# Attention scores by heads and weight transposes by token halves, each in one row half of the matrix array

## The chip, the cores and the metric

The kernel runs on one core of one Trainium2 chip. The metric is the device time of one execution in microseconds, lower is better. Five things work side by side on the core: TensorE (PE; its weight loads are listed as PEld), VectorE (DVE), ScalarE (ACT), GpSimd (POOL), and the DMA queue that SyncE (SP) feeds.

## What is computed

An attention whose keys and values are averaged over groups of 8 positions is followed by a mixture layer with a rational activation and by a gated layer. Only the attention is touched here:

```
q, k, v: (8 batches, 8 heads, 576 positions, 64)
k_p = k.reshape(8, 8, 72, 8, 64).mean(axis=3)      # 72 pooled keys
v_p = v.reshape(8, 8, 72, 8, 64).mean(axis=3)
scores = 1/8 * q @ k_p^T                           # 576 x 72 for each head
attn = exp(scores - max); attn = attn / (sum(attn) + 1e-09)
x = attn @ v_p                                     # to (4608 tokens, 512)
h = x @ w_in; g = P(h) / Q(h); y = g @ w_out       # 512 -> 2048 -> 512
out = (sigmoid(y @ w_gate) * (y @ w_val)) @ w_out2 # 512 -> 1536 -> 512
```

## The kernel before

The 4608 tokens are 36 tiles of 128 and 9 blocks of 512. A batch has 576 = 4.5 x 128 tokens, so that 4 of the 36 tiles hold halves of two batches ("two-part tiles") and there are 40 tile parts. For each part, `tile_attention` (L549) does the following:

- **Scores** (L565 to L569, tile `sc`): four fp32 matmuls, one for each pair of heads. The stationary operand is the query tile (128 rows, two heads of 64 each, by 128 tokens). The moving operand is `kbd` (128 rows x 144), in which the pooled keys of the two heads stand as a block diagonal with zeros elsewhere. `place_keys` (L470) copies the pooled keys `kp` into `kbd` for each batch, by four ACT instructions (L476), and one DVE memset (L733) has set its zeros. Two matmuls fill one PSUM bank, two banks make a part. The profile lists each fp32 matmul as two records, so a part has 8.
- **Softmax**: for each bank a maximum (L574) and a subtraction (L575) on DVE, then exp on ACT, a sum and a reciprocal on DVE, a product on POOL. The result `e` has 128 tokens as rows.
- **Transposes** (L594, tile `pta`): eight a tile, one for each head, of 128 tokens x 72 weights against the 128 x 128 identity. Each is one record. Four fill one bank, and ACT copies each bank to `aT` (L596).
- **Weights times values** (L610, tile `psx`): fp32 matmuls with 72 rows and 64 stationary columns. The two heads of a pair write to the lower and the upper 64 PSUM partitions, so each uses one column half of the array.

The mixture layer runs between these pieces: `h` and `acc` at L628 to L630, 12 matmuls of 512 columns for `h` and 12 for `acc` in each of 144 steps. The blocks' attention is spread over the steps of the block ahead. What stands where on each engine is fixed before the launch: `Planner.order` (L109) starts tasks by rank as engines and buffers come free under estimated costs, and the program is emitted in that order. Attention uses the same four PSUM banks as `h` (slot list `h`), at most three at a time. The gated layer begins when all this is done, at about 830 us.

Of the kernel before, what the change touches and what calls it, by code (L numbers as in the profile page):

```python
# [13 lines left out]
AF = mybir.ActivationFunctionType  # L14
ALU = mybir.AluOpType
AX = mybir.AxisListType
# [172 lines left out]
def attention_moe_glu_kernel(ctx: ExitStack, tc: tile.TileContext, q, k, v, w_in, w_out, ca, cb, w_gate, w_val, w_out2, out):  # L189
    nc = tc.nc  # L190
# [42 lines left out]
    slots = {"W": [f"w{i}" for i in range(NF1 + FS + NR)], "ST": [f"st{i}" for i in range(6)],  # L233
             "h": [f"b{i}" for i in range(4)], "su": [f"su{i}" for i in range(3)], "y": [f"y{i}" for i in range(3)],
             "m": [f"m{i}" for i in range(3)], "g": [f"g{i}" for i in range(3)], "xs": ["xs0", "xs1"],
             "raw": [f"raw{i}" for i in range(3)], "e": ["e"], "aT": ["aT"], "kp": ["kp"], "vp": ["vp"],
             "vh": ["vh0", "vh1"], "kbd": ["kbd"]}
    slots.update({f"acc{e}": [f"b{4 + e}"] for e in range(NJ)})
    slots.update({n: [n] for n in ("mx0", "mx1", "r0", "r1", "wqt")})
    for n in ("A11", "S2", "S3", "S1", "A12", "A22", "S4"):  # L240
# [206 lines left out]
    def tmp_where(blk, own):  # L447
        return [own, "W"] if blk <= 1 else [own]

    def small(shape, name, where, kind=None):  # L450
        return Buf(name, shape, F32, where, kind)

    kbd = small([P, NJ, 2, SP], "kbd", ["kbd"])
    vh, xs, rawq, turned, pooled = {}, {}, {}, [], {}

    def k_cols(c):
# [2 lines left out]
    def keys(b, rank, rank_load):  # L459
# [6 lines left out]
            plan("DVE", dve(m * POOL), rank, lambda raw=raw, m=m, cols=cols: nc.vector.reduce_sum(  # L466
                kp.t[:, cols], raw.t[:, :m * POOL].rearrange("p (s j) -> p s j", j=POOL), axis=AX.X), w=[(kp, c)], r=[raw])
        pooled[b] = kp

    def place_keys(b, rank):  # L470
        kp = pooled.pop(b)
        for js, cs in ((slice(0, NJ // 2), (0, 1, 2)), (slice(NJ // 2, NJ), (2, 3, 4))):
            for e in range(2):
                half = slice(e * D, (e + 1) * D)
                def fn(e=e, js=js, half=half):
                    nc.scalar.activation(kbd.t[half, js, e], kp.t.rearrange("p (j s) -> p j s", s=SP)[half, js], AF.Copy)  # L476
                plan("ACT", act(SP * 2), rank, fn,
                    w=[(kbd, (js.start, e))], r=[(kp, c) for c in cs])

    def values0(rank, rank_load):  # L480
        vp = small([P, NCH, D], "vp", ["vp"])
# [68 lines left out]
    def tile_attention(i, rank, gate_on=[]):  # L550
        parts = units[i]
        blk, o = divmod(i * P, TB)
        raw = rawq[i]
        kind = None if blk == 0 else "ha"
        own = ["h"] if blk else ["h", "acc0", "acc1", "acc2"]
        mx = small([P, H], "mx", [f"mx{i % 2}"])
        e_ = small([P, H, SP + 1], "e", tmp_where(blk, "e"), "tmp" if blk < 2 else None)
        plan("POOL", 0.15, rank, lambda: nc.gpsimd.memset(e_.t[:, :, SP:], 1e-9), w=[(e_, 2)])

        for x, (b, n) in enumerate(parts):  # L560
            rows = slice(x * n, (x + 1) * n)
            if i == first[b]:
                place_keys(b, rank)
            for g in range(2):
                sc = psum("sc", own, kind)  # L565

                def fn(g=g, sc=sc):
                    for j in (2 * g, 2 * g + 1):
                        nc.tensor.matmul(sc.t[:, (j % 2) * 2 * SP:(j % 2 + 1) * 2 * SP], raw.t[:, j * P:(j + 1) * P], kbd.t[:, j].rearrange("p e s -> p (e s)"), start=True, stop=True)  # L569
                plan("PE", 0.5, rank, fn, w=[sc], r=[raw, (kbd, (2 * g, 0)), (kbd, (2 * g, 1))],  # L570
                     after=(turned[-1:] if blk > 1 else turned[-3:-2]) + gate_on)
                hs = slice(4 * g, 4 * g + 4)
                scv = lambda sc=sc, rows=rows: sc.t[rows, :4 * SP].rearrange("p (h s) -> p h s", s=SP)
                plan("DVE", dve(288) - 0.04, rank, lambda hs=hs, scv=scv, rows=rows: nc.vector.reduce_max(mx.t[rows, hs], scv(), axis=AX.X), w=[(mx, (g, x))], r=[sc])  # L574
                plan("DVE", dve(288) - 0.04, rank, lambda hs=hs, scv=scv, rows=rows, n=n: nc.vector.tensor_tensor(  # L575
                    out=e_.t[rows, hs, :SP], in0=scv(), in1=mx.t[rows, hs].unsqueeze(2).to_broadcast([n, 4, SP]), op=ALU.subtract),
                    w=[(e_, (g, x))], r=[sc, (mx, (g, x))])
        plan("ACT", act(576), rank, lambda: nc.scalar.activation(e_.t[:, :, :SP], e_.t[:, :, :SP], AF.Exp, scale=scale / POOL),
             w=[(e_, (g, x)) for g in range(2) for x in range(len(parts))])
        r = small([P, H], "r", [f"r{i % 2}"])  # L580

        def fn():
            nc.vector.reduce_sum(r.t, e_.t, axis=AX.X)
            nc.vector.reciprocal(r.t, r.t)
        plan("DVE", 0.85, rank, fn, w=[r], r=[e_])
        plan("POOL", 1.12, rank, lambda: nc.gpsimd.tensor_tensor(
            out=e_.t[:, :, :SP], in0=e_.t[:, :, :SP], in1=r.t.unsqueeze(2).to_broadcast([P, H, SP]), op=ALU.mult), w=[e_], r=[r])
        aT = small([P, H, P], "aT", tmp_where(blk, "aT") + (["ST"] if blk >= 2 else []), "tmp" if blk < 2 else None)
        for g in range(2):
            pta = psum("pta", own, kind)  # L590

            def fn(g=g, pta=pta):
                for h in range(4 * g, 4 * g + 4):
                    nc.tensor.transpose(pta.t.rearrange("p (h t) -> p h t", t=P)[:SP, h % 4], e_.t[:, h, :SP], ident)  # L594
            pt = plan("PE", 0.44, rank, fn, w=[pta], r=[e_])
            plan("ACT", act(512) - 0.08, rank, lambda g=g, pta=pta: nc.scalar.activation(  # L596
                aT.t[:SP, 4 * g:4 * g + 4], pta.t.rearrange("p (h t) -> p h t", t=P)[:SP], AF.Copy), w=[(aT, g)], r=[pta])
        turned.append(pt)
        waiting.append((i, parts, aT))
        if blk >= 2 and i % 2 == 0:  # L600
            return
# [127 lines left out]

    T0 = -20.0  # L730
    values_at = {}
    for c in range(1):
        plan("DVE", 0.6, T0, lambda: nc.vector.memset(kbd.t, 0.0), w=[kbd])  # L733
    warm = psum("warm", ["acc2"])

    def fn():
# [54 lines left out]
    for n in range(N1):  # L791
# [6 lines left out]
        x = n - last_step  # L798
        if x == BX:
            bar = plan("-", 0.0, n, "late", after=[t for t in plan.tasks if any(b.where and b.where[0] in  # L800
                       ("ST", "raw", "e", "aT", "kp", "vp", "vh", "kbd", "mx0", "mx1", "r0", "r1") for b in t.bufs)])
            rawx[0] = Buf("rawx", [P, 8 * TB], F32, ["xs"])
            for h, d, ib, o, m in x_pieces(0):
                load(n, 4 * m / 2, lambda h=h, d=d, ib=ib, o=o, m=m: nc.sync.dma_start(x_dst(h, d, m), x2d[ib].t[:, :, o:o + m]),
                     w=[(rawx[0], (h, d))], r=[x2d[ib]], after=first_mm[-1:])
# [24 lines left out]
    with tc.manual_schedule():  # L830
# [4 lines left out]
        sm = att.enter_context(tc.tile_pool(name="sm", bufs=1))  # L835
        stage = att.enter_context(tc.tile_pool(name="stage", bufs=1))
        stage_t.append(stage.tile([P, len(slots["ST"]) * 8 * P], F32, name="stage"))
        pools.update(w=wp, b=ps, su=rot, y=rot, m=rot, g=g_p, xs=xs_p, raw=raw_p, e=ap1, aT=ap1, kp=ap1, vp=ap1, vh=ap1, kbd=ap1,
                     mx=sm, r=sm)
        for t in jobs:  # L840
            if t.fn == "late":
# [358 lines left out]
```

## Time and profile before

| | |
|---|---|
| median of 3 runs | 1736.67 us (1735.71 to 1737.2) |
| profiled execution, its own time | 1734.64 us |
| its span, first to last instruction | 1732.6 us |
| PE busy | 1709.0 us (99%) |
| ACT busy, DVE busy | 1046.6 us (60%), 1235.0 us (71%) |
| chain that ended last, share of PE | 93% |
| granted TensorE clock, mean | 0.996 |

A PE record lasts longer than its turn, since matmuls are pipelined: a 512-column matmul is listed with some 390 ns and the next one starts 227 ns behind it. So costs on PE are read from start to start, and busy times of small matmuls can't be added up.

### The profile page before, as it was taken

To read this page: it belongs to the slowest core of one execution; us is meant where nothing else is said; L and a number is where in the kernel's file an instruction comes from. 1 tells how busy PE (TensorE), PEld (TensorE's weight loads), DVE (VectorE), ACT (ScalarE), POOL (GpSimd) and SP (SyncE) were. 2 spreads that over 40 slices of the span, in tenths; PEclk is the share of its full clock that TensorE was granted. 3 is DMA by queue.
4 is the path that set the end of the run, shared out by engine and by line. 5 is a ranking of instruction groups with operands and counts; after the bars stand their busy time and mean duration, and the time that the engine had idled before them with its cause. 6 is when DMAs were issued, how large, how long until landed. Compare 5 with 4: busy or idle time off the path is not lost.

```text
span 1732.6 us, 28635 instructions
## 1 busy us (share of the span) xinstructions
PE 1709.0 (99%) x10044; PEld 1553.5 (90%) x10044; DVE 1235.0 (71%) x2146; ACT 1046.6 (60%) x1957; POOL 730.0 (42%) x807
## 2 busy tenths in 40 slices
PE   7899999999999999999999999999999999999999
PEld 6688888888888888788889999999999999999999
DVE  7898888888887878788786466466466467457456
ACT  6999778787877878898885244244244234235234
POOL 6675356454644646777544320330330330330320
PEclk9999999999999999999999999999999999999999
DMA  7675463545535446775753998888888888888856
GB/s 242 190 278 197 158 192 127 177 145 181 187 116 184 146 157 187 227 239 185 235 181 120 301 317 279 277 265 279 272 272 280 277 265 279 272 270 279 255 181 207
DMA packets 180867, 384.61 MB, mean 222 GB/s; under 512 B 24692, under 2 KB 92276, under 8 KB 180724
## 3 DMA queue, kind: packets, MB, share of 16 engines
q1 hardware_dynamic: 180724, 382.78, 67.4%
q8 instruction: 80, 1.31, 0.3%
q14 instruction: 63, 0.52, 0.1%
HBM read 322.96 MB, written 58.72 MB: 220 GB/s over the span
## 4 chain that ended last, share of the span: by engine, by line
PE 93%; ACT 2%; DMA 1%; DVE 1%; POOL 1%; issue 0%; SPq 0%; POOLq 0%; ACTq 0%
PE h L628 17%; PE h L630 17%; PE h L629 17%; PE acc L628 7%; PE acc L630 7%; PE acc L629 7%; PE acc L1044 5%; PE acc L1043 5%; PE acc L1042 5%; PE sc L569 2%; PE psx L610 2%; PE pta L594 2%; DMA stage<-in_moe_w_in_dram 0%; ACT stage L296 0%; DMA rawv<-in_v_dram 0%
## 5 line engine op out<-in xcount | busy, mean ns | idle before, releaser
L933 DVE TENSOR_TENSOR t<-h,t 128x384 f32<-128x384 f32 x360 | 200.8, 558 | 251.2 <-PE h L630 123.0
L668 POOL TENSOR_TENSOR g<-y,g 128x512 fp32r<-128x512 f32 x143 | 186.6, 1305 | 205.3 <-ACT g L666 175.7
L1002 POOL TENSOR_TENSOR ga<-t 128x384 f32<-128x384 f32 x48 | 48.9, 1019 | 452.5 <-DVE t L933 445.6
L628 PE MATMUL h<-xs,wi 128*128 128x512 f32 x576 | 228.9, 397 | 5.7 <-ACT aT L596 3.6
L628 PE MATMUL acc<-g,wo 128*128 128x512 f32 x576 | 230.1, 399 | 0.0
L630 PE MATMUL acc<-g,wo 128*128 128x512 f32 x576 | 225.2, 391 | 1.9 <-POOL g L668 1.9
L630 PE MATMUL h<-xs,wi 128*128 128x512 f32 x576 | 225.3, 391 | 0.0
L629 PE MATMUL h<-xs,wi 128*128 128x512 f32 x576 | 225.2, 391 | 0.0
L629 PE MATMUL acc<-g,wo 128*128 128x512 f32 x576 | 224.6, 390 | 0.0
L1044 PE MATMUL acc<-wo,go 128*128 128x256 f32 x756 | 213.9, 283 | 0.0
L1043 PE MATMUL acc<-wo,go 128*128 128x256 f32 x756 | 213.9, 283 | 0.0
L1042 PE MATMUL acc<-wo,go 128*128 128x256 f32 x756 | 213.9, 283 | 0.0
L628 PE MATMUL h<-xS,wq 128*128 128x384 f32 x576 | 192.4, 334 | 0.0
L630 PE MATMUL h<-xS,wq 128*128 128x384 f32 x576 | 192.4, 334 | 0.0
L629 PE MATMUL h<-xS,wq 128*128 128x384 f32 x576 | 192.4, 334 | 0.0
L947 ACT ACTIVATE t<-h 128x384 f32<-128x384 f32 x72 | 35.3, 491 | 242.2 <-PE h L630 238.4
L662 DVE SCALAR_TENSOR_TENSOR y<-y,coef,h 128x512 f32<-128x512 f32 x144 | 107.2, 744 | 70.9 <-ACT h L661 70.5
L1044 PEld LDWEIGHTS acc<-wo,go 128*128 128x128 f32 x756 | 145.1, 192 | 0.0
L1043 PEld LDWEIGHTS acc<-wo,go 128*128 128x128 f32 x756 | 145.1, 192 | 0.0
L1042 PEld LDWEIGHTS acc<-wo,go 128*128 128x128 f32 x756 | 145.1, 192 | 0.0
L628 PE MATMUL h<-xA,wq 128*128 128x384 f32 x432 | 144.3, 334 | 0.0
L629 PE MATMUL h<-xA,wq 128*128 128x384 f32 x432 | 144.3, 334 | 0.0
(129 smaller groups left out, 4258.1 us busy)
## 6 DMA issues: line engine op xcount, KB each, us to landing
wq<-w2d SPq DMA_DIRECT2D x252, 512.0 KB
wo<-wo2d SPq DMA_DIRECT2D x126, 512.0 KB
wo<-wod SPq DMA_DIRECT2D x96, 512.0 KB
w2d<-stage SPq DMA_DIRECT2D x36, 512.0 KB
wo2d<-stage SPq DMA_DIRECT2D x84, 128.0 KB
rawk<-in_k_dram SPq DMA_DIRECT2D x32, 256.0 KB
rawq<-in_q_dram SPq DMA_DIRECT2D x32, 256.0 KB
rawv<-in_v_dram SPq DMA_DIRECT2D x32, 256.0 KB
```

The costliest lines, as they stand in the source:

```text
L569: nc.tensor.matmul(sc.t[:, (j % 2) * 2 * SP:(j % 2 + 1) * 2 * SP], raw.t[:, j * P:(j + 1) * P], kbd.t[:, j].rearrange("p e s -> p (e s)"), ...
L628: nc.tensor.matmul(out_, wl, xh, start=start, stop=False, skip_group_check=on)
L629: nc.tensor.matmul(out_, wh, xh, start=False, stop=False, skip_group_check=on)
L630: nc.tensor.matmul(out_, wh, xl, start=False, stop=stop, skip_group_check=on)
L662: plan("DVE", 0.66, rank, lambda: STT(out=y.t, in0=y.t, scalar=coef[:, 0:1], in1=h.t, op0=ALU.add, op1=ALU.mult), w=[y], r=[h])
L668: plan(on, cost, rank, lambda: eng.tensor_tensor(out=g.t[:, 1], in0=y.t, in1=g.t[:, 0].bitcast(F32), op=ALU.subtract), w=[(g, 1)], r=[y, ( ...
L933: nc.vector.tensor_tensor(out=out_, in0=a, in1=b, op=ALU.add)
L947: nc.scalar.activation(t["u"], b[1], AF.Copy)
L1002: eng.tensor_tensor(out=dst, in0=x, in1=y, op=ALU.mult)
L1042: nc.tensor.matmul(a, gh, wh, start=s_ == 0 and not on, stop=False, skip_group_check=on)
L1043: nc.tensor.matmul(a, gh, wl, start=False, stop=False, skip_group_check=on)
L1044: nc.tensor.matmul(a, gl, wh, start=False, stop=s_ == NS - 1, skip_group_check=on)
```

## The change

**Scores by heads.** Each matmul takes one head: 64 rows of the query tile (the even head of a pair lies on partitions 0 to 63, the odd one on 64 to 127), all 128 tokens as stationary columns, and 72 pooled keys read from `kp` itself as moving columns. A part has 8 matmuls, 16 records. Even heads write one PSUM bank, odd heads another, and they alternate. `kbd`, its memset and the copies on ACT are gone; `kp` has two buffers. DVE's maximum and subtraction take every second head (`slice(g, H, 2)`).

**Transposes by token halves.** Each head's transpose is cut into tokens 0 to 63 and 64 to 127, with 64 rows and a 64 x 64 identity. A tile has 16 in place of 8. The halves alternate and have a bank each. ACT's copy writes 64 of every 128 columns of `aT`.

Scores of a part, and transposes of a tile, are now one PE task each that takes two banks at once. Their planned costs are 0.6 and 0.55 us, where two tasks had 0.5 and 0.44 us each.

```
-            if i == first[b]:
-                place_keys(b, rank)
+            sc = [psum("sc", own, kind) for _ in range(2)]
+
+            def fn(b=b, sc=sc):
+                for j in range(NJ):
+                    for g in range(2):
+                        nc.tensor.matmul(sc[g].t[:, j * SP:(j + 1) * SP], raw.t[g * D:(g + 1) * D, j * P:(j + 1) * P],
+                                         pooled[b].t[g * D:(g + 1) * D, j * SP:(j + 1) * SP], start=True, stop=True)
+            plan("PE", 0.6, rank, fn, w=sc, r=[raw, pooled[b]],
+                 after=(turned[-1:] if blk > 1 else turned[-3:-2]) + gate_on)
             for g in range(2):
-                sc = psum("sc", own, kind)
-
-                def fn(g=g, sc=sc):
-                    for j in (2 * g, 2 * g + 1):
-                        nc.tensor.matmul(sc.t[:, (j % 2) * 2 * SP:(j % 2 + 1) * 2 * SP], raw.t[:, j * P:(j + 1) * P], kbd.t[:, j].rearrange("p e s -> p (e s)"), start=True, stop=True)
-                plan("PE", 0.5, rank, fn, w=[sc], r=[raw, (kbd, (2 * g, 0)), (kbd, (2 * g, 1))],
-                     after=(turned[-1:] if blk > 1 else turned[-3:-2]) + gate_on)
-                hs = slice(4 * g, 4 * g + 4)
+                hs = slice(g, H, 2)
...
+        pta = [psum("pta", own, kind) for _ in range(2)]
+
+        def fn(pta=pta):
+            for h in range(H):
+                for g in range(2):
+                    rows = slice(g * D, (g + 1) * D)
+                    nc.tensor.transpose(pta[g].t.rearrange("p (h t) -> p h t", t=D)[:SP, h], e_.t[rows, h, :SP], ident[rows, rows])
+        pt = plan("PE", 0.55, rank, fn, w=pta, r=[e_])
         for g in range(2):
-            pta = psum("pta", own, kind)
-
-            def fn(g=g, pta=pta):
-                for h in range(4 * g, 4 * g + 4):
-                    nc.tensor.transpose(pta.t.rearrange("p (h t) -> p h t", t=P)[:SP, h % 4], e_.t[:, h, :SP], ident)
-            pt = plan("PE", 0.44, rank, fn, w=[pta], r=[e_])
             plan("ACT", act(512) - 0.08, rank, lambda g=g, pta=pta: nc.scalar.activation(
-                aT.t[:SP, 4 * g:4 * g + 4], pta.t.rearrange("p (h t) -> p h t", t=P)[:SP], AF.Copy), w=[(aT, g)], r=[pta])
+                aT.t[:SP, :, g * D:(g + 1) * D], pta[g].t.rearrange("p (h t) -> p h t", t=D)[:SP], AF.Copy), w=[(aT, g)], r=[pta[g]])
```

On PE, at a place in the mixture layer's second block, the program before has two half tasks of transposes and one task of scores with full-array matmuls (`acc<-g,wo`) between them:

```order
L594 MATMUL pta<-ident,e 72x128 x4
L628 MATMUL acc_2133<-g,wo_2028 128x512
L629 MATMUL acc_2133<-g,wo_2028 128x512
L630 MATMUL acc_2133<-g,wo_2028 128x512
L594 MATMUL pta<-ident,e 72x128 x4
L628 MATMUL acc_2139<-g,wo_2028 128x512
L629 MATMUL acc_2139<-g,wo_2028 128x512
L630 MATMUL acc_2139<-g,wo_2028 128x512
L569 MATMUL sc<-kbd,rawq 128x144 x4
```

The changed program has at the corresponding place (names as above, lines 9 to 13 lower):

```order
L584 MATMUL pta<-ident,e 72x64 x16
L619 MATMUL acc_2226<-g,wo_2210 128x512
L620 MATMUL acc_2226<-g,wo_2210 128x512
L621 MATMUL acc_2226<-g,wo_2210 128x512
L619 MATMUL acc_2233<-g,wo_2210 128x512
L620 MATMUL acc_2233<-g,wo_2210 128x512
L621 MATMUL acc_2233<-g,wo_2210 128x512
L556 MATMUL sc<-kp,rawq 128x72 x8
```

Both kinds of half-array work still stand singly between full-array matmuls. From the block 2 tiles on there are 31 groups of scores and 28 of transposes, and none of them touches another or a `psx` group.

On ACT, at the very beginning of the program before (`e` is the exp, `aT` the copies of the transposes, `stage` weight conversion):

```order
L476 ACTIVATE kbd<-kp 64x2x72 x4
L578 ACTIVATE e<-e 128x8x72 x2
L596 ACTIVATE aT<-pta 72x512 x2
L296 ACTIVATE stage<-stage 128x512
L578 ACTIVATE e<-e 128x8x72
L596 ACTIVATE aT<-pta 72x512 x2
L298 ACTIVATE stage<-stage 128x512
```

And in the changed program:

```order
L567 ACTIVATE e<-e 128x8x72 x2
L587 ACTIVATE aT<-pta 72x8x64 x2
L296 ACTIVATE stage<-stage 128x512
L567 ACTIVATE e<-e 128x8x72
L298 ACTIVATE stage<-stage 128x512
L587 ACTIVATE aT<-pta 72x8x64 x2
```

The key copies are gone, and a stage conversion has moved ahead of the second tile's copies; the other engines' early rows are rearranged in the same way.

## Rows read from the trace of the kernel before

**Rows 1.** Page of the profile: the chain that ended last, by engine

```profile
PE 93%; ACT 2%; DMA 1%; DVE 1%; POOL 1%; issue 0%; SPq 0%; POOLq 0%; ACTq 0%
```

**Rows 2.** Busy time by stretch: stretch, its length, busy us of each engine (instructions)

```profile
0.00:60.00 60.00, 46.84 (x329) 39.48 (x330) 46.98 (x91) 41.21 (x78) 37.05 (x63) 0.89 0.73 236
...
107.40:830.00 722.60, 720.05 (x3753) 598.55 (x3754) 597.17 (x988) 589.03 (x1057) 412.44 (x488) 1.00 0.54 179
```

**Rows 3.** The last chain in order of time, start and length, some pieces ahead of 107.4

```profile
43.32 0.67 ACT stage L296
...
94.02 1.44 DVE stage L299
...
107.40 0.50 PE acc L630
```

**Rows 4.** PE groups by form, 107.4 to 830 us: records | busy us, mean ns | idle before

```profile
L569 PE MATMUL sc<-kbd,rawq 128*128 128x144 f32 x248 | 35.9, 285 | 0.0
L594 PE MATMUL pta<-ident,e 128*72 128x128 f32 x224 | 29.5, 272 | 0.0
...
L610 PE MATMUL psx<-stage,vh 72*64 72x64 f32 x64 | 2.2, 222 | 0.0
```

**Rows 5.** PE in order of time, transposes then scores: start, us to the last end

```profile
207.33 1.03 PE L594 MATMUL pta<-ident,e 128*72 128x128 f32 x8
...
208.44 0.40 PE L629 MATMUL acc<-g,wo 128*128 128x512 f32 x1
...
208.91 1.14 PE L569 MATMUL sc<-kbd,rawq 128*128 128x144 f32 x8
...
210.12 0.40 PE L629 MATMUL h<-xs,wi 128*128 128x512 f32 x1
```

**Rows 6.** PE in order of time, two groups of weights times values

```profile
211.72 0.39 PE L630 MATMUL h<-xs,wi 128*128 128x512 f32 x1
...
212.40 0.39 PE L630 MATMUL h<-xs,wi 128*128 128x512 f32 x1
212.72 1.10 PE L610 MATMUL psx<-aT,vh 72*64 72x128 f32 x16
213.65 1.04 PE L610 MATMUL psx<-stage,vh 72*64 72x128 f32 x16
214.62 0.50 PE L628 MATMUL acc<-g,wo 128*128 128x512 f32 x1
214.96 0.39 PE L629 MATMUL acc<-g,wo 128*128 128x512 f32 x1
```

**Rows 7.** Small fp32 matmuls with 64 moving columns, in order of time

```profile
277.35 1.10 PE L610 MATMUL psx<-stage,vh 72*64 72x64 f32 x32
...
20.03 1.40 PE L511 MATMUL vps<-vp,sel 128*72 128x64 f32 x19
```

**Rows 8.** Those matmuls and the weight loads by form, whole run: busy us, mean ns

```profile
L511 PE MATMUL vps<-vp,sel 128*72 128x64 f32 x22 | 1.6, 228 | 0.0
...
L594 PEld LDWEIGHTS pta<-ident,e 128*72 128x72 f32 x288 | 31.8, 117 | 13.6 <-POOL e L586 6.1 <-ACT aT L596 1.9 <-issue 0.3
...
L610 PEld LDWEIGHTS psx<-stage,vh 72*64 72x64 f32 x256 | 13.0, 137 | 0.0
...
L511 PEld LDWEIGHTS vps<-vp,sel 128*72 128x72 f32 x22 | 1.6, 145 | 0.0
```

**Rows 9.** PE around the two records with 64 rows, from three narrow looks

```profile
21.33 0.43 PE L511 MATMUL vps<-vp,sel 128*72 128x64 f32 x2
...
21.49 0.34 PE L511 MATMUL vps<-vp,sel 64*72 64x64 f32 x2
...
21.60 0.23 PE L511 MATMUL vps<-vp,sel 64*72 64x64 f32 x1
```

**Rows 10.** ACT's key copies (L476) up to 107.4 us: ns min/median/max, first and last start

```profile
L476 ACT ACTIVATE kbd<-kp x8: 316/323/325, 7.2 to 32.8; 64x144 f32<-64x144 f32 x8
```

**Rows 11.** PE's waits, whole run: us in total, times, longest us

```profile
PE h L628 <- ACT aT L596: 3.6, 2, 2.6
```

More of the change, by code (lines that the diff above doesn't have):

```diff
@@ L235, in attention_moe_glu_kernel @@
              "m": [f"m{i}" for i in range(3)], "g": [f"g{i}" for i in range(3)], "xs": ["xs0", "xs1"],
-             "raw": [f"raw{i}" for i in range(3)], "e": ["e"], "aT": ["aT"], "kp": ["kp"], "vp": ["vp"],
-             "vh": ["vh0", "vh1"], "kbd": ["kbd"]}
+             "raw": [f"raw{i}" for i in range(3)], "e": ["e"], "aT": ["aT"], "kp": ["kp0", "kp1"], "vp": ["vp"],
+             "vh": ["vh0", "vh1"]}
     slots.update({f"acc{e}": [f"b{4 + e}"] for e in range(NJ)})
@@ L451, in small @@
         return Buf(name, shape, F32, where, kind)
-    kbd = small([P, NJ, 2, SP], "kbd", ["kbd"])
     vh, xs, rawq, turned, pooled = {}, {}, {}, [], {}
@@ L468, in keys @@
         pooled[b] = kp
[L470 to L478, printed above, removed]
     def values0(rank, rank_load):
@@ L561, in tile_attention @@
             rows = slice(x * n, (x + 1) * n)
-            if i == first[b]:
-                place_keys(b, rank)
-            for g in range(2):
-                sc = psum("sc", own, kind)
-                def fn(g=g, sc=sc):
-                    for j in (2 * g, 2 * g + 1):
-                        nc.tensor.matmul(sc.t[:, (j % 2) * 2 * SP:(j % 2 + 1) * 2 * SP], raw.t[:, j * P:(j + 1) * P], kbd.t[:, j].rearrange("p e s -> p (e s)"), start=True, stop=True)
-                plan("PE", 0.5, rank, fn, w=[sc], r=[raw, (kbd, (2 * g, 0)), (kbd, (2 * g, 1))],
-                     after=(turned[-1:] if blk > 1 else turned[-3:-2]) + gate_on)
-                hs = slice(4 * g, 4 * g + 4)
-                scv = lambda sc=sc, rows=rows: sc.t[rows, :4 * SP].rearrange("p (h s) -> p h s", s=SP)
-                plan("DVE", dve(288) - 0.04, rank, lambda hs=hs, scv=scv, rows=rows: nc.vector.reduce_max(mx.t[rows, hs], scv(), axis=AX.X), w=[(mx, (g, x))], r=[sc])
+            sc = [psum("sc", own, kind) for _ in range(2)]
[6 more added lines that the diff above has]
+                 after=(turned[-1:] if blk > 1 else turned[-3:-2]) + gate_on)
+            for g in range(2):
+                hs = slice(g, H, 2)
+                scv = lambda sc=sc[g], rows=rows: sc.t[rows, :4 * SP].rearrange("p (h s) -> p h s", s=SP)
+                plan("DVE", dve(288) - 0.04, rank, lambda hs=hs, scv=scv, rows=rows: nc.vector.reduce_max(mx.t[rows, hs], scv(), axis=AX.X), w=[(mx, (g, x))], r=[sc[g]])
                 plan("DVE", dve(288) - 0.04, rank, lambda hs=hs, scv=scv, rows=rows, n=n: nc.vector.tensor_tensor(
                     out=e_.t[rows, hs, :SP], in0=scv(), in1=mx.t[rows, hs].unsqueeze(2).to_broadcast([n, 4, SP]), op=ALU.subtract),
-                    w=[(e_, (g, x))], r=[sc, (mx, (g, x))])
+                    w=[(e_, (g, x))], r=[sc[g], (mx, (g, x))])
         plan("ACT", act(576), rank, lambda: nc.scalar.activation(e_.t[:, :, :SP], e_.t[:, :, :SP], AF.Exp, scale=scale / POOL),
@@ L731, in attention_moe_glu_kernel @@
     values_at = {}
-    for c in range(1):
-        plan("DVE", 0.6, T0, lambda: nc.vector.memset(kbd.t, 0.0), w=[kbd])
     warm = psum("warm", ["acc2"])
@@ L800, in attention_moe_glu_kernel @@
             bar = plan("-", 0.0, n, "late", after=[t for t in plan.tasks if any(b.where and b.where[0] in
-                       ("ST", "raw", "e", "aT", "kp", "vp", "vh", "kbd", "mx0", "mx1", "r0", "r1") for b in t.bufs)])
+                       ("ST", "raw", "e", "aT", "kp", "vp", "vh", "mx0", "mx1", "r0", "r1") for b in t.bufs)])
             rawx[0] = Buf("rawx", [P, 8 * TB], F32, ["xs"])
@@ L837, in attention_moe_glu_kernel @@
         stage_t.append(stage.tile([P, len(slots["ST"]) * 8 * P], F32, name="stage"))
-        pools.update(w=wp, b=ps, su=rot, y=rot, m=rot, g=g_p, xs=xs_p, raw=raw_p, e=ap1, aT=ap1, kp=ap1, vp=ap1, vh=ap1, kbd=ap1,
+        pools.update(w=wp, b=ps, su=rot, y=rot, m=rot, g=g_p, xs=xs_p, raw=raw_p, e=ap1, aT=ap1, kp=ap1, vp=ap1, vh=ap1,
                      mx=sm, r=sm)
```

## The prediction

> **What bounds the kernel now.** I began with the chain that ended last: 93% of it is PE [rows 1]. A mean over stages says little, so I then read the stretches. From 107.4 to 830 us, where blocks 2 to 8 get their attention beside the mixture layer, PE is busy for 720.05 of 722.60 us at full clock [rows 2]. There a nanosecond saved or added on PE is one of the run. Ahead of 107.4 us it is otherwise: the chain runs over ACT, DVE and transfers and comes to PE only at 107.40 [rows 3], and in the first 60 us PE is busy for 46.84 us [rows 2]. There PE work has cover. From 830 us on nothing is changed.
>
> So the sum is made from the stretch 107.4 to 830. It has 248 records of scores, 31 groups of 8, and 224 transposes, 28 groups of 8 [rows 4]. What a group takes is read from start to start. The regular step of a 512-column matmul is (212.40 - 211.72)/3 = 0.227 us [rows 6]. From the first transpose to the second matmul behind the group are 208.44 - 207.33 = 1.11 us, less one step 0.88; for scores 210.12 - 208.91 - 0.227 = 0.98 [rows 5]. One record after the other this is, from the spans of the groups and the record durations, (1.03 - 0.272)/7 = 0.108 us for a transpose and (1.14 - 0.285)/7 = 0.122 for a score record [rows 4, 5]. Eight of each are 0.87 and 0.98, the whole group: between full-array work these groups pay nothing for entering and leaving.
>
> **The change: what half-array pairs can do.** The trace has no two row halves side by side, but it has two column halves: `psx`. Its second 16 records span 1.04 us [rows 6]; less the 0.27 that a record with 128 moving columns lasts (0.272 for a transpose [rows 4]) these are seven steps of 0.11, 0.109 closer by, for each pair: as much as one transpose with the same moving columns takes alone. So two halves of the array run at the same time there. I take row halves to do the same. The other bound is that they take turns.
>
> **Transposes.** A pair has 64 moving columns in place of 128. The nearest row is the `psx` pair with 64 moving columns: 32 records in 1.10 us, less the last record's 0.222, over 15 steps, 0.058 us a pair [rows 4, 7]. The bounds are 0.054 (half of 0.108) and 0.116 (two turns of 0.058). At 0.058 a group falls from 0.87 to 0.46, and 28 groups save 11.4 us.
>
> **Scores.** A pair streams only 72 columns for 144 before, which by the columns would be 0.061 us. But each half still loads 128 stationary columns, and loads set the pace of small matmuls here. `vps` has the same 64 moving columns as the two-part `psx` and 72 stationary columns for 64, and goes at (1.40 - 0.228)/18 = 0.065 us a record [rows 7, 8]; eight more loaded columns cost 0.007 us, 0.84 ns a column. Load durations give the same slope: 145 against 137 ns is 1.0 ns a column [rows 8]. A load of 128 columns then needs 0.058 + 64 x 0.00084 = 0.112 us, against 0.122 now. Bounds are 0.061 and 0.224 (loads in turns). I take 0.112, since both rows with short streams lie on that line: 31 x 8 x 0.010 = 2.5 us saved. Halving the streamed columns buys almost nothing.
>
> The Trainium skill (TensorEngine Tiling (Array Packing), Overview, Theoretical Speedup) promises up to 2x where the contraction is 64 or less. By it both pairs would halve, and the two savings would be 31 x 0.49 + 28 x 0.44 = 27 us in place of 14. The slope of the load rows speaks against it for scores.
>
> **The switches.** `psx` pays for its halves at both ends. In [rows 6] from 212.40 to 214.96 are 2.56 us; less two regular steps and 16 pairs of 0.109 (1.74), 0.36 us are left. They lie at the entry (212.40 to 212.72 is 0.09 over a step, the first group is 0.06 longer than 8 pairs) and at the exit (213.65 to 214.62 is 0.10 over 8 pairs, 214.62 to 214.96 is 0.11 over a step). That rows cost the same is seen once: before the two `vps` records with 64 rows, the start comes 0.16 us after the one before, where 0.065 is regular, and the next after 0.11 [rows 9]. These are 0.14 over, as at the entry of `psx`. The loads of the new shape are not fetched early. So a group of scores, with 128 columns to load for 64, pays 0.05 more than `psx`, 0.41 us; a transpose, whose load takes 117 against 137 ns [rows 8], some 0.34. The order shows the changed groups standing singly among full-array matmuls, so every one pays: 31 x 0.41 + 28 x 0.34 = 22.2 us. The bounds are 0 and 0.46 a group (the longer load at the exit too).
>
> The same page of the Trainium skill (Key Properties) says that changing the tiling mode drains TensorE. It gives no price; the 0.36 us is the trace's.
>
> **What lies off the path.** The key copies on ACT are 8 of 0.323 us ahead of 107.4 us, 2.6 us [rows 10], at 7.2 and up to 32.8 us; the chain there passes over other work. Later copies lie beside a busy PE. The memset stood ahead of the first keys on DVE, which wait for their transfer. DVE's and ACT's reads keep their element counts. The two banks are taken together, but PE will need 1.3 us for a group of scores and 0.8 for one of transposes where 0.6 and 0.55 are planned, so the banks are sooner free than asked for. The early stretch is rearranged on all engines, and pays its switches behind waits. I set it at 0, with bounds of -5 and +5.
>
> **Sum.** 22.2 - 2.5 - 11.4 = +8.3 us on the profiled execution's 1734.64 (2.04 of which lie outside its span) gives 1742.9. That execution was 2.03 under the median, so the prediction is 1745.0 us, 0.5% slower.
>
> **Rivals.**
> 1. *Loads don't bind in row halves.* A score pair at 0.061 saves 31 x 8 x 0.061 = 15.1 us: +22.2 - 15.1 - 11.4 = -4.3, 1732.4. For it: each half loads only 64 rows. Against: `psx` halves also load half the array and lie on the line of `vps`. The 2x of the Trainium skill (TensorEngine Tiling (Array Packing), Theoretical Speedup) would come to this here once the switches are paid.
> 2. *Row switches are free.* Then -13.9, 1722.8, faster. It decides from 0.24 us a group downwards, where the two savings outweigh 59 switches. Against: [rows 9], where one entry has its full price.
> 3. *Row halves take turns*: scores +31 x 8 x 0.102 = 25.3, transposes +28 x 8 x 0.008 = 1.8, switches 22.2: +49, 1786. For it: no row shows two row halves at once, and both write the same PSUM partitions, though in different banks, while the `psx` halves write different ones.
> 4. *The early stretch gives the gain.* If all 2.6 us of copies were on its path, and the 2.6 us for which `h` waits for ACT's `aT` copy [rows 11] go too, 5.2 us come off: 1739.8, within the bound.
>
> **How the numbers follow.** The forecast gets 0.58 (its own range 1738 to 1752, from the early stretch and 0.3 to 0.46 a switch), rival 1 0.12, rival 2 0.08, rival 3 0.12, rival 4 0.10. The range 1730 to 1757 leaves out rivals 2 and 3, 0.20. About 0.2% (3.5 us) is what a measurement of this kernel can tell from no change, so faster ends at 1733.2 and same at 1740.1. Faster: rival 2, most of rival 1 and a little of the rest, 0.19. Same: rival 4, the rest of rival 1 and the lower edge of the forecast, 0.19. Slower: 0.62.
>
> **What would show it.** In the profile after, from 107 to 830 us: pairs of transposes 0.058 us apart and of scores 0.11; 0.32 us and not 0.23 from a full-array matmul to the first record of a group; 0.34 and not 0.23 behind the first matmul after it; the gated layer beginning some 8 us later. Score pairs at 0.06 would be rival 1, at 0.22 rival 3, groups without longer steps at their ends rival 2, and a first 107 us shorter by 5 us rival 4. New waits of PE for banks (`h` or `sc` behind DVE or ACT) beyond 5 us in all would make the forecast wrong from above.

## The result: 0.6% slower, with the profile after

| | before | after |
|---|---|---|
| median of the runs side by side | 1736.40 us (6 runs) | 1746.94 us (6 runs, 1744.45 to 1747.52) |
| ratio, 95% interval | | 1.0059 (1.0046 to 1.0072) |
| profiled execution, its own time | 1734.64 us | 1746.48 us |
| its span | 1732.6 us | 1744.4 us |

The ratio is 10.2 us; the two profiled executions are 11.8 us apart. The prediction was 1745.0 us, 8.3 us slower.

The page of the profile after, busy time of the engines and the chain by engine:

```profile
PE 1718.9 (99%) x10652; PEld 1542.0 (88%) x10652; DVE 1236.4 (71%) x2145; ACT 1033.7 (59%) x1925; POOL 730.2 (42%) x807
...
PE 91%; DVE 3%; ACT 2%; DMA 2%; issue 1%; POOL 1%; SPq 0%; POOLq 0%; ACTq 0%
```

PE still holds the chain (93% before, [rows 1]). ACT has 13 us less to do, most of it key copies, and no time is seen to come of it.

The stretches of after, with the columns of [rows 2]:

```profile
0.00:60.00 60.00, 46.49 (x408) 40.17 (x410) 41.42 (x85) 35.78 (x64) 33.68 (x61) 0.74 0.72 231
...
107.40:830.00 722.60, 717.43 (x4190) 577.75 (x4189) 597.86 (x981) 574.03 (x1020) 407.27 (x480) 1.00 0.54 177
```

In the second stretch PE is as full as before, 717.43 of 722.60 us at full clock. In the first 60 us the granted clock is 0.74 where it was 0.89.

PE groups by form in after, 107.4 to 830 us, to be held against [rows 4]:

```profile
L556 PE MATMUL sc<-kp,rawq 64*128 64x72 f32 x496 | 34.6, 279 | 0.0
L584 PE MATMUL pta<-ident,e 64*72 64x64 f32 x448 | 18.2, 220 | 0.1
```

Twice the records, 31 groups of 16 scores and 28 of 16 transposes. What a group takes is read in order of time, a group of scores:

```profile
303.81 0.39 PE L620 MATMUL h<-xs,wi 128*128 128x512 f32 x1
304.04 0.39 PE L621 MATMUL h<-xs,wi 128*128 128x512 f32 x1
304.36 1.12 PE L556 MATMUL sc<-kp,rawq 64*128 64x72 f32 x16
305.40 0.50 PE L619 MATMUL acc<-g,wo 128*128 128x512 f32 x1
305.74 0.39 PE L620 MATMUL acc<-g,wo 128*128 128x512 f32 x1
```

and one of transposes:

```profile
316.19 0.39 PE L621 MATMUL h<-xs,wi 128*128 128x512 f32 x1
316.51 0.64 PE L584 MATMUL pta<-ident,e 64*72 64x64 f32 x16
317.08 0.50 PE L619 MATMUL acc<-g,wo 128*128 128x512 f32 x1
317.42 0.39 PE L620 MATMUL acc<-g,wo 128*128 128x512 f32 x1
```

Entry into a group takes 0.32 us where a regular step has 0.23. From the start of the last matmul ahead to the start of the second one behind, less two regular steps of 0.227, the scores take 305.74 - 304.04 - 0.45 = 1.25 us and the transposes 0.78 us (1.248 and 0.772 by the single records). Before it was 0.98 and 0.88 ([rows 5], counted from a first record that starts one regular step behind). In the single records of these groups the pairs stand 0.1117 and 0.0558 us apart. So eight pairs of scores are 0.894 us and 0.354 us of the group are entering and leaving; for transposes 0.446 and 0.325 us.

PE's waits in after behind 107.4 us, us in total, times, longest:

```profile
PE h L619 <- DVE y L655: 3.2, 3, 1.1
PE h L619 <- DVE e L564: 1.4, 1, 1.4
PE acc L621 <- POOL g L659: 1.1, 2, 0.7
PE acc L619 <- ACT o L683: 0.9, 1, 0.9
```

They are 6.6 us in all. The first row was 0.3 us before. Its three waits stand behind the groups of scores at 262.75 (a two-part tile), 565.78 and 666.80 us (whole tiles). At the first of them, all engines of after in order of time:

```profile
262.75 1.11 PE L556 MATMUL sc<-kp,rawq 64*128 64x72 f32 x16
...
263.90 0.81 DVE L563 TENSOR_REDUCE mx<-sc 64x4 f32<-64x288 f32 x2 [1.21 <-PE sc L556]
...
267.15 0.67 DVE L655 SCALAR_TENSOR_TENSOR y<-h,y 128x512 f32<-128x512 f32 x1
...
267.88 0.50 PE L619 MATMUL h<-xs,wi 128*128 128x512 f32 x1 [1.06 <-DVE y L655]
...
268.40 0.44 DVE L564 TENSOR_TENSOR e<-sc,mx 64x288 f32<-64x288 f32 x1
```

The group takes two of the four banks at 262.75. DVE takes the maxima of both banks, then six operations of the mixture layer, and comes to the subtraction that empties the first bank at 268.40, 5.65 us later; meanwhile `h` has to wait for a bank that DVE's `y` gives back. At the other two waits the subtraction comes 5.65 us behind the group's start as well. The same part in before, where both banks are taken at 262.47 too, one task right behind the other:

```profile
262.47 1.14 PE L569 MATMUL sc<-kbd,rawq 128*128 128x144 f32 x8
...
264.19 0.44 DVE L575 TENSOR_TENSOR e<-sc,mx 64x288 f32<-64x288 f32 x1
```

There the first subtraction comes after 1.72 us. Over the 31 parts of before the median is 1.75 us and the longest 4.24.

### The profile page after: what moved, and what is told of

It reads as the page before. It is cut to its first block, busy times and chain, and to the rows that moved or that the text cites. A ratio compares the mean times of both kernels' runs of the same rounds, so it can differ in the third digit from the quotient of the medians.

```text
span 1744.4 us, 29804 instructions
## 1 busy us (share of the span) xinstructions
PE 1718.9 (99%) x10652; PEld 1542.0 (88%) x10652; DVE 1236.4 (71%) x2145; ACT 1033.7 (59%) x1925; POOL 730.2 (42%) x807
## 4 chain that ended last, share of the span: by engine, by line
PE 91%; DVE 3%; ACT 2%; DMA 2%; issue 1%; POOL 1%; SPq 0%; POOLq 0%; ACTq 0%
PE h L619 17%; PE h L621 17%; PE h L620 17%; PE acc L619 7%; PE acc L621 7%; PE acc L620 7%; PE acc L1033 5%; PE acc L1032 5%; PE acc L1031 5%; PE sc L556 2%; PE psx L601 2%; PE pta L584 1%; DMA rawq<-in_q_dram 1%; DMA stage<-in_moe_w_out_dram 0%; DVE u L647 0%
## 5 line engine op out<-in xcount | busy, mean ns | idle before, releaser
L645 ACT ACTIVATE u<-h,coef 128x512 f32<-128x512 f32 x144 | 98.8, 686 | 81.2 <-PE h L621 80.4
L619 PE MATMUL h<-xA,wq 128*128 128x384 f32 x432 | 144.3, 334 | 0.0
```

What stands on the lines that cost most here:

```text
L619: nc.tensor.matmul(out_, wl, xh, start=start, stop=False, skip_group_check=on)
L645: ACT(0.57, rank, lambda: nc.scalar.activation(u.t, h.t, AF.Abs, scale=coef[:, 5:6]), w=[u], r=[h, coef_b])
```

## The ledger that the experiments are read by

In every trace the same piece of work can be found: the 145th `h` matmul, at 114.56 us before, and the first matmul with 384 columns, with which the gated layer begins, at 927.39 before and 939.20 after. Behind it nothing changes: the difference of 11.8 us stays to the end of the span. Between the two marks each step on PE beyond a regular one was put down to what stood there (group costs as above). The columns behind the ratio are us, worked out from the single records of the profiled execution and given as differences to before. Before itself has 31.30 for scores (31 parts), 25.94 for transposes (28 tiles) and 4.07 for waits and other steps. `psx` groups cost 29.6 us with little change. One profiled execution need not lie at the median: e2's, at 1735.19 us, is the fastest of eleven, e6's, at 1768.61, the slowest of five. The four terms add up to the delay of the gated layer within 0.8 us, mostly since a matmul more or less stands ahead of the first mark; in e9, e5, e12 and e6 `psx` and mixed groups add 0.5 to 2.2.

| kernel | median us | ratio to before (95%) | gated layer later | by the mark at 114 | scores | transposes | waits, other steps |
|---|---|---|---|---|---|---|---|
| after | 1746.94 | 1.0059 (1.0046 to 1.0072) | 11.8 | 2.1 | 8.8 | -4.0 | 5.5 |
| e1_scores_only | 1746.85 | 1.0072 (1.0059 to 1.0084) | 11.7 | 1.4 | 8.0 | -1.1 | 3.4 |
| e2_transposes_only | 1737.88 | 1.0014 (1.0005 to 1.0023) | 0.5 | 0.4 | 3.4 | -4.1 | 1.5 |
| e3_tasks_only | 1745.38 | 1.0061 (1.0047 to 1.0075) | 10.4 | 4.9 | 0.7 | -0.3 | 5.8 |
| e4_halves_in_turn | 1772.35 | 1.0215 (1.0197 to 1.0234) | 37.0 | 7.6 | 23.9 | 3.0 | 3.3 |
| e6_real_costs | 1763.44 | 1.0174 (1.0160 to 1.0188) | 34.1 | 17.1 | 7.4 | -3.8 | 12.9 |
| e9_tasks_real_costs | 1740.54 | 1.0034 (1.0021 to 1.0046) | 4.5 | -1.3 | 1.1 | 1.0 | 1.5 |
| e7_full_first | 1754.96 | 1.0129 (1.0114 to 1.0145) | 19.6 | 5.5 | 14.1 | -4.0 | 4.6 |
| e8_full_between | 1766.13 | 1.0188 (1.0173 to 1.0204) | 31.1 | 6.0 | 24.9 | -4.0 | 4.8 |
| e11_full_same_order | 1735.69 | 1.0008 (0.9999 to 1.0016) | 1.7 | -0.4 | 0.5 | -1.0 | 3.2 |
| e12_before_low_costs | 1749.54 | 1.0085 (1.0073 to 1.0097) | 12.6 | 3.5 | 2.3 | -1.2 | 8.2 |
| e10_transposes_real_cost | 1745.89 | 1.0064 (1.0052 to 1.0076) | 11.9 | 6.3 | 4.1 | -2.8 | 4.3 |
| e5_wider_keys | 1745.46 | 1.0064 (1.0050 to 1.0079) | 10.8 | 0.8 | 8.8 | -4.0 | 4.9 |

## The experiments

The prediction's theory was that the array itself costs the time: switches against pairs. Rival B: the new tasks, which take two banks at once, and the order that the planner makes of them. Rival C: planned costs that are too low, so that PE comes late to what the planner lined up.

### The two halves of the change apart

**Scores alone.** The transposes of after are put back as before, two tasks a tile, of four full-array transposes and one bank each:

```
-        pta = [psum("pta", own, kind) for _ in range(2)]
...
+            pta = psum("pta", own, kind)
...
+                    nc.tensor.transpose(pta.t.rearrange("p (h t) -> p h t", t=P)[:SP, h % 4], e_.t[:, h, :SP], ident)
+            pt = plan("PE", 0.44, rank, fn, w=[pta], r=[e_])
```

> Scores by heads in row halves as in the change, transposes full-array as before. Theory A (array and switches: in the trace of the changed kernel a score group takes 8 pairs of 0.112 plus 0.354 us for entering and leaving, 1.25 in all, against 0.98 before): 31 groups from 107 to 830 us lose 0.27 each, 8.4 us, so about 1745 us (1741 to 1749). Theory B (the array work is not to blame; tasks that take two PSUM banks at once and the smaller planned costs rearrange the program, and that costs the 10.5 us): half the tasks are changed here, about 1742. In the profile A wants score groups of 1.25 us and no more waits of PE than in the changed kernel.

**Transposes alone.** The scores, `kbd`, its memset and the key copies are as before:

```
+                    nc.scalar.activation(kbd.t[half, js, e], kp.t.rearrange("p (j s) -> p j s", s=SP)[half, js], AF.Copy)
...
+                        nc.tensor.matmul(sc.t[:, (j % 2) * 2 * SP:(j % 2 + 1) * 2 * SP], raw.t[:, j * P:(j + 1) * P], kbd.t[:, j].rearrange("p e s -> p (e s)"), start=True, stop=True)
+                plan("PE", 0.5, rank, fn, w=[sc], r=[raw, (kbd, (2 * g, 0)), (kbd, (2 * g, 1))],
```

> Transposes by token halves as in the change, scores with block-diagonal keys as before. Theory A: a transpose group takes 8 pairs of 0.056 plus 0.325 us, 0.77, against 0.87 before; 28 groups gain 0.10 each, 2.8 us: about 1734 us (1730 to 1738, the early stretch open). Theory B (two-bank tasks cost the time): about 1742.

Scores alone are 0.72% slower, 12.5 us, as much as the whole change or a little more. Transposes alone are 0.14% slower, 2.4 us (0.5 in the profiled execution), where the array ought to give some microseconds back. In the ledger it does, 4.1 us; but the score groups, which are those of before, cost 3.4 us more (35 groups for 34; what PE waits at a group's first record counts with the group), and 1.5 us go to other waits. So the order of the work around an edit moves as much as the edit. That made rival B worth a run of its own.

**The tasks alone.** Before, with full-array matmuls, but each part's scores and each tile's transposes in one task with two banks and the planned costs of after:

```
-                plan("PE", 0.5, rank, fn, w=[sc], r=[raw, (kbd, (2 * g, 0)), (kbd, (2 * g, 1))],
+            plan("PE", 0.6, rank, fn, w=sc, r=[raw] + [(kbd, (2 * g, e)) for g in range(2) for e in range(2)],
...
-            pt = plan("PE", 0.44, rank, fn, w=[pta], r=[e_])
+        pt = plan("PE", 0.55, rank, fn, w=pta, r=[e_])
```

> All matmuls and transposes full-array as before, but planned as in the change: one task for a part's scores and one for a tile's transposes, each with two banks at once and with the planned costs 0.6 and 0.55. Theory A: only the rearrangement of the program is left, which in the changed kernel's profile accounts for what array work and switches don't, 10.5 - 5.6 = 5 us: between 1736 and 1742. Theory B: 1746, as the changed kernel.

Without one half-array matmul the kernel is 0.61% slower, as slow as the change. Taken alone this would make rival B the whole cause. The ledger says otherwise: e3 loses 4.9 us ahead of 114 us and 5.8 in waits, and nothing in its groups; after loses 8.8 us in its score groups. Two different losses of the same size. The largest of PE's waits behind 107.4 us in e3 is the one seen in after:

```profile
PE h L629 <- DVE y L665: 2.7, 3, 0.9
```

**Halves in turn.** The loops of after exchanged, so that all records of one half come first, then all of the other:

```
-                for j in range(NJ):
-                    for g in range(2):
+                for g in range(2):
+                    for j in range(NJ):
...
-            for h in range(H):
-                for g in range(2):
+            for g in range(2):
+                for h in range(H):
```

> The changed kernel with all work of the lower half issued before that of the upper half, in scores and transposes, so that pairs can't run side by side. Theory A (side by side is what keeps the pairs at 0.112 and 0.056 us): 16 score records in turn take 1.79 for 0.89 us, 31 x 0.90 = 28 us more, transposes 0.89 for 0.45, 28 x 0.45 = 12 more, about 1787 us. If the two halves' loads or streams are independent of the order of issue: 1747, no change. If only the loads overlap and matmuls never did: 1747 too, with single records 0.056 us apart.

It is 2.15% slower, 25 us more than after, and less than two full turns would cost. PE of e4 in order of time, a group of each kind:

```profile
310.08 0.90 PE L584 MATMUL pta<-ident,e 64*72 64x64 f32 x16
310.91 0.50 PE L619 MATMUL acc<-g,wo 128*128 128x512 f32 x1
...
315.21 1.62 PE L556 MATMUL sc<-kp,rawq 64*128 64x72 f32 x16
316.76 0.50 PE L619 MATMUL acc<-g,wo 128*128 128x512 f32 x1
```

The 16 score records span 1.62 us for 1.12 in after. One half by itself goes no faster than a pair: the records of the lower half stand 0.112 us apart. So the pairs of after do run at the same time in both halves. That the span isn't twice as long has its reason in the starts of the single records:

```
lower half (issued first)  315.213 .379 .491 .603 .714 .826 .938 316.049
upper half (issued behind) 315.720 .887 .998 316.110 .222 .333 .445 .557
```

The trace doesn't name the half. The records are told apart by their two trains of 0.112 us steps, and the one at 315.720 carries a semaphore wait, as in after the second record of a group does, the upper half's first. So the upper half begins while three records of the lower one have yet to start.

### Planned costs

**The change planned at what it costs.**

```
-            plan("PE", 0.6, rank, fn, w=sc, r=[raw, pooled[b]],
+            plan("PE", 1.25, rank, fn, w=sc, r=[raw, pooled[b]],
...
-        pt = plan("PE", 0.55, rank, fn, w=pta, r=[e_])
+        pt = plan("PE", 0.78, rank, fn, w=pta, r=[e_])
```

> The changed kernel, planned with the prices that its trace shows: 1.25 us for a group of scores and 0.78 for one of transposes in place of 0.6 and 0.55. Theory C (the planned costs are too low, so the program is ordered for a PE that is ahead of the real one, and its waits from 107 us on, 7 to 8 us in the changed kernel against 3 before, come from that): they fall to about 3, total about 1742 us. Theory D (two banks taken at once make the waits, whatever the plan says): they stay, 1746 to 1748. Array work is the same in both.

**The tasks of e3 planned at what they cost.**

```
-            plan("PE", 0.6, rank, fn, w=sc, r=[raw] + [(kbd, (2 * g, e)) for g in range(2) for e in range(2)],
+            plan("PE", 1.0, rank, fn, w=sc, r=[raw] + [(kbd, (2 * g, e)) for g in range(2) for e in range(2)],
...
-        pt = plan("PE", 0.55, rank, fn, w=pta, r=[e_])
+        pt = plan("PE", 0.88, rank, fn, w=pta, r=[e_])
```

> Full-array work in two-bank tasks, as in the run with tasks only, but planned at 1.0 and 0.88 us, which is what this work takes. Theory C: the extra waits go, about 1736 to 1739 us. Theory D: 1744 to 1746, as with the low planned costs.

The two go opposite ways: by the medians e9 is 4.8 us faster than e3, e6 16.5 us slower than after (before, run beside each of them, had medians of 1734.4 to 1736.4 us). In e6 the groups cost what they cost in after, and the loss is in the order: 17.1 us ahead of 114 us, and waits that after doesn't have. PE's waits of e6 behind 107.4 us:

```profile
PE h L619 <- DVE wi L310: 5.6, 1, 5.6
PE acc L621 <- POOL g L659: 4.4, 4, 2.3
PE h L619 <- ACT aT L587: 4.0, 1, 4.0
```

The first is for a weight conversion on DVE (`wi`), which the new order brings late. Rival C falls as a rule.

**Before with low planned costs.** Only two numbers of before are changed, so that a part or a tile has the planned sum of after:

```
-                plan("PE", 0.5, rank, fn, w=[sc], r=[raw, (kbd, (2 * g, 0)), (kbd, (2 * g, 1))],
+                plan("PE", 0.3, rank, fn, w=[sc], r=[raw, (kbd, (2 * g, 0)), (kbd, (2 * g, 1))],
...
-            pt = plan("PE", 0.44, rank, fn, w=[pta], r=[e_])
+            pt = plan("PE", 0.275, rank, fn, w=[pta], r=[e_])
```

> The kernel before, one-bank tasks and full-array work, planned at half of the changed kernel's costs for each task, 0.3 and 0.275 us in place of 0.5 and 0.44. With the two runs of two-bank tasks this makes a square of bank taking and planned costs. If the low costs do the harm in the order: 1739 to 1745 us. If taking two banks does: 1735 to 1737.

**Transposes alone, planned at their cost.** In e2:

```
-        pt = plan("PE", 0.55, rank, fn, w=pta, r=[e_])
+        pt = plan("PE", 0.78, rank, fn, w=pta, r=[e_])
```

> Only the transposes in row halves, planned at the 0.78 us that they take in place of 0.55. Array work gains 0.10 x 28 = 2.8 us. The order decides the rest, which moved the other pairs of planned costs by -5 and by +16 us: 1732 if it is no worse than before, 1738 to 1745 if it is as with the low cost or worse.

Two numbers in a plan cost the kernel before 0.85%, more than the change does, with the same instructions on one bank each. PE's waits of e12 behind 107.4 us are spread over several kinds:

```profile
PE acc L630 <- POOL g L668: 2.3, 4, 1.1
PE h L628 <- DVE e L575: 2.2, 3, 1.0
PE acc L628 <- ACT g L666: 2.1, 1, 2.1
```

And e10, with the truer number, is 8.0 us slower than e2. Truer costs gave -4.8, +8.0 and +16.5 us, lower ones in before +14.7. There is no direction in it. Why one order is good and the next bad stays open.

### The switch and the load, each by itself

**A full-array product ahead of the group, and the same in its middle.** One product of 128 rows, whose result is overwritten by the pairs; first against after, then the second against the first:

```
             def fn(b=b, sc=sc):
+                nc.tensor.matmul(sc[0].t[:, 2 * SP:3 * SP], raw.t[:, 2 * P:3 * P], pooled[b].t[:, 2 * SP:3 * SP], start=True, stop=True)
                 for j in range(NJ):
```

```
             def fn(b=b, sc=sc):
-                nc.tensor.matmul(sc[0].t[:, 2 * SP:3 * SP], raw.t[:, 2 * P:3 * P], pooled[b].t[:, 2 * SP:3 * SP], start=True, stop=True)
                 for j in range(NJ):
+                    if j == 2:
+                        nc.tensor.matmul(sc[0].t[:, 2 * SP:3 * SP], raw.t[:, 2 * P:3 * P], pooled[b].t[:, 2 * SP:3 * SP], start=True, stop=True)
```

> The changed kernel with one more full-array fp32 matmul (72 moving columns, 128 loaded) ahead of each group of scores, into a region that the group then overwrites. It adds two records of 0.112 us to a group and no switch: 31 x 0.22 = 7 us from 107 to 830 us, total about 1754 us. All theories agree; it is the base for the next.

> The same extra matmul in the middle of each group, between the fourth and the fifth half-array matmul. Theory A (entering and leaving half-array work costs 0.35 us whatever the amount of work): one more exit and entry in each group, 31 x 0.35 = 11 us over the run with the matmul ahead, about 1765 us. If the longer steps at the groups' ends are not the switch but the wait for banks or weights of the next task: no more than 1 to 2 us over it.

The two have the same work in every group; e8 leaves the half arrays and comes back once more. PE of e7 in order of time, a group:

```profile
309.12 0.34 PE L554 MATMUL sc<-kp,rawq 128*128 128x72 f32 x2
309.39 1.11 PE L557 MATMUL sc<-kp,rawq 64*128 64x72 f32 x16
310.43 0.50 PE L620 MATMUL acc<-g,wo 128*128 128x512 f32 x1
```

and of e8:

```profile
312.34 0.67 PE L558 MATMUL sc<-kp,rawq 64*128 64x72 f32 x8
312.94 0.44 PE L556 MATMUL sc<-kp,rawq 128*128 128x72 f32 x2
313.31 0.67 PE L558 MATMUL sc<-kp,rawq 64*128 64x72 f32 x8
313.91 0.50 PE L621 MATMUL acc<-g,wo 128*128 128x512 f32 x1
```

In e7 the full records stand ahead of the one entry; in e8 they part the group into two, each with its own entry and exit. The ledger gives 56.23 - 45.41 = 10.8 us for 31 more switches, 0.349 us each; the medians give 11.2 us, 0.36 each. That agrees with the 0.354 us found in the groups of after. The switch is shown by itself, and its size too.

**Wider keys.** 104 moving columns for 72, with the same loads (the columns beyond a head's 72 are overwritten by the next head):

```
+                        to = min(j * SP + 104, NJ * SP)
+                        nc.tensor.matmul(sc[g].t[:, j * SP:to], raw.t[g * D:(g + 1) * D, j * P:(j + 1) * P],
+                                         pooled[b].t[g * D:(g + 1) * D, j * SP:to], start=True, stop=True)
```

> The changed kernel with 104 in place of 72 moving columns in three of four score matmuls (the surplus columns are overwritten by the next matmul). Theory A (the load of 128 columns sets a pair's 0.112 us; 104 columns stream in 0.087): no change, 1746 to 1748, pairs still 0.112 apart. If streaming sets the pace: 12 of 16 records get 44% longer, 0.112 to 0.16 for six pairs of eight, 31 x 0.29 = 9 us more, 1756.

A group of e5, PE in order of time:

```profile
303.10 1.11 PE L557 MATMUL sc<-kp,rawq 64*128 64x104 f32 x16
304.14 0.50 PE L620 MATMUL acc<-g,wo 128*128 128x512 f32 x1
```

It is 1.04 us from the first record to the next matmul, as in after (304.36 to 305.40), and the 31 groups cost 40.10 us in both. Three of four heads stream 44% more columns at no cost, so the moving columns don't set the pace of the pairs. That the loads of 128 stationary columns do is what is left, and what the line of `psx` and `vps` gave beforehand; no run changed the stationary columns.

### The order of after with full-array work

This run separates the array from the order. Every instruction stands where after has it, on all engines, with the same tasks, planned costs and two banks, and without `kbd` and the key copies; only the 8 half-array products become 4 full ones, and the 16 half transposes 8 full ones. The run leaves out the block diagonal of `kbd`, so that the scores of two heads are mixed: the same work on other values.

```
-                    for g in range(2):
-                        nc.tensor.matmul(sc[g].t[:, j * SP:(j + 1) * SP], raw.t[g * D:(g + 1) * D, j * P:(j + 1) * P],
-                                         pooled[b].t[g * D:(g + 1) * D, j * SP:(j + 1) * SP], start=True, stop=True)
+                    o = (j % 2) * 2 * SP
+                    nc.tensor.matmul(sc[j // 2].t[:, o:o + 2 * SP], raw.t[:, j * P:(j + 1) * P],
+                                     pooled[b].t[:, o:o + 2 * SP], start=True, stop=True)
...
-                for g in range(2):
-                    rows = slice(g * D, (g + 1) * D)
-                    nc.tensor.transpose(pta[g].t.rearrange("p (h t) -> p h t", t=D)[:SP, h], e_.t[rows, h, :SP], ident[rows, rows])
+                nc.tensor.transpose(pta[h // 4].t.rearrange("p (h t) -> p h t", t=P)[:SP, h % 4], e_.t[:, h, :SP], ident)
```

> The program of the changed kernel instruction for instruction and in its order on every engine, but with full-array matmuls and transposes of the sizes before (the scores of a pair of heads are left mixed, since no block diagonal is built: the same work, other values). What is left against the kernel before is the new order and the two-bank tasks alone. Theory A, with the array part taken from the traces (scores +0.27 x 31, transposes -0.10 x 28): 1746.9 - 5.6 = 1741 us. If the order makes all of the loss: 1747. If the array work makes all of it: 1736.

It takes 1735.69 us, 0.08% over before, with an interval that holds no change. So the order and the two-bank tasks of after, with the key copies gone, cost about nothing (0.9 us by the medians, 1.7 in the profiled executions), and rival B falls: what e3 lost, it lost in another order. A group of scores of e11, PE in order of time:

```profile
299.81 0.39 PE L619 MATMUL h<-xs,wi 128*128 128x512 f32 x1
300.04 1.14 PE L556 MATMUL sc<-kp,rawq 128*128 128x144 f32 x8
300.92 0.49 PE L617 MATMUL acc<-g,wo 128*128 128x512 f32 x1
301.25 0.40 PE L618 MATMUL acc<-g,wo 128*128 128x512 f32 x1
```

It costs 301.25 - 299.81 - 0.45 = 0.98 us, as before. The waits of after for `y` are there too, 0.4 us shorter:

```profile
PE h L617 <- DVE y L653: 2.8, 3, 0.9
PE acc L619 <- POOL g L657: 1.1, 2, 0.7
```

After minus e11 is what half arrays do in a fixed order: 10.1 us in the profiled executions, 8.9 by the ratios (1.0059/1.0008). It divides into scores +8.3, transposes -3.0, ahead of 114 us +2.5, waits and other steps +2.3.

## Why the prediction was right, and where it wasn't

**PE's time is the run's time: right.** The delay of the gated layer is the delay of the end, to the tenth of a microsecond. One slip without consequence: the gated layer begins at 927 us, not at 830; only mixture steps lie between.

**Two row halves run at the same time: right.** Pairs of transposes are 0.0558 us apart (0.058 predicted). Rival 3, in which they take turns, falls; where the order of issue makes them take turns for the most part, in e4, it costs 25 us.

**Loads bind the scores: right as far as tested.** Pairs are 0.1117 us apart (0.112 predicted), for 72 or 104 moving columns; the load itself was not varied. Each load of 64 rows and 128 columns lasts 187 ns in after, and a full one of 128 rows 0.19 us: half the rows are no shorter to load. The Trainium skill (TensorE: Matmul & The Clock Gate, LDWEIGHTS) has that rule, that columns count and rows don't; this trace agrees. Rival 1 falls, and with it the factor of two for the scores.

**Every group pays a switch: right, a little too dear.** Rival 2 falls by e8. A group of scores pays 0.354 us where 0.41 were put; the 0.05 us added for its longer load is not there, and the price of `psx` (0.36, [rows 6]) would have done. A group of transposes pays 0.325 for 0.34. A part of the price can be seen at the entry: in all 59 groups of after the first load starts with its matmul (304.356 and 304.357 us in the group above), while in e11 and before it starts some 0.23 us ahead of it. The Trainium skill (TensorEngine Tiling (Array Packing), Key Properties) says that a change of mode drains TensorE; the 0.349 us of a switch in e8 fit this, but no run shows the drain itself.

**The array's sum: +5.3 in place of +8.3 us.** Switches are 31 x 0.354 + 28 x 0.325 = 20.1 us (22.2 predicted); scores save 31 x (0.983 - 0.894) = 2.8 (2.5), transposes 28 x (0.876 - 0.446) = 12.0 (11.4), with full-array groups as e11 has them. That leaves +5.3, and the ledger has +8.3 - 3.0 = +5.3.

**The early stretch at nothing: wrong by 2 us.** It loses 2.1 us against before and 2.5 against e11. PE had been thought to hide its switches behind waits. The stretch of after from 14 to 20 us:

```profile
14.00:20.00 6.00, 6.00 (x72) 5.83 (x71) 4.34 (x11) 3.55 (x7) 3.64 (x9) 0.50 0.95 333
```

PE is busy throughout, at 0.50 of full clock, that is the 1.2 GHz level, with scores and transposes of the first tiles. In the 6 us ahead it was busy for 2.87 us, at 0.59. In e11 the same 6 us have 0.82, and the 6 us ahead of them 3.12 us of work at 0.90:

```profile
14.00:20.00 6.00, 6.00 (x53) 5.62 (x51) 4.68 (x13) 4.03 (x8) 3.49 (x8) 0.82 0.90 325
```

How much of the 2.5 us is the clock was not tried apart. e5 has the order of after, a mean clock of 0.83 in its first 60 us for 0.74, and loses 0.8 us there and not 2.1. That is not the chance of one execution: over the whole run all six executions of after have a mean clock of 0.991 to 0.992, all three of e5 0.993 to 0.994. Why after's is lower stays open. The opposite bound, rival 4, in which the key copies give 5 us back, falls.

**No new waits: wrong.** "The banks are sooner free than asked for" is the step that failed. It looked at how long PE holds a bank. It is DVE that gives them back, and in three groups of after the first subtraction comes 5.65 us behind the start of the scores, at most 4.24 us in before. Taking two banks at once is not in itself the difference, since in 28 of 31 parts before took both within 0.5 us too; it is where the planner puts the subtraction on DVE. Subtractions later than 5 us go with two-bank score tasks for the most part: e1, e3, e9, e11 and after have two to four, before, e2 and e12 none, e10 one. The price is 1.7 us of order in e11 (waits and other steps +3.2, the rest gains), and 2.3 more in after, of which the waits for `y` make 0.4 and one for ACT's `o` 0.9; the rest stays open. The mark set for it, more than 5 us of new waits for banks behind DVE or ACT, was not met: 4.6 us, where before had 1.2.

**The time.** 5.3 + 2.5 + 2.3 + 1.7 = 11.8 us, the difference of the profiled executions, for a forecast of 8.3. The sign and about half of the loss were the array's, by the mechanism forecast. That the time came out within 2 us owes something to two errors of opposite sign: the array 3.0 too dear, and 6.5 us of order and early work at nothing.

One of the marks was no mark. The 0.34 us behind the first matmul after a group, meant to show a switch, stands in e11 too (300.92 to 301.25, 0.33 us), where nothing is switched. The group as a whole shows it; a single step doesn't.

## What to carry to other kernels

Splitting small matmuls over row halves pays where the moving columns set the pace, as in the transposes (0.0558 us for 0.108), and not where they don't, as in the scores with their 128 stationary columns (0.112 for 0.122); and each group that stands alone between full-array work pays 0.35 us, so that it must save more than that. Where a planner orders the work, compare an operation with another in the same order, as after with e11: two planned numbers moved this kernel by 15 us with no instruction changed, and e3 by itself would have put the blame in the wrong place. Of a bank that is taken early, ask which engine gives it back and when that engine comes to it, not how long the engine that fills it needs.

## What the chip showed that was not expected

- PE starts matmuls out of their issued order across row halves: in e4 the upper half's first record starts at 315.720 us, ahead of the lower half's last three, issued before it. The Trainium skill (TensorE: Matmul & The Clock Gate, The mechanism) says that matmuls start strictly in program order; here the measurement differs.
- Row halves cost the same to enter and leave as the column halves of `psx`: 0.354 and 0.325 us against 0.36. The load of 128 columns, twice that of `psx`, adds nothing that can be seen.
